# Moving the next pass's k times v products from inside the first MLP to the border between the two MLPs

## The chip, the cores and the metric

One of the cores of a Trainium2 chip runs the whole program. The metric is the time of one execution on the device in microseconds (us); the kernel before is given by the median of three runs.

## What is computed

Linear attention with a norm, and then two MLPs over the same 4608 tokens, all in float32:

```python
kv = np.einsum('bhsd,bhse->bhde', k, v)
out = np.einsum('bhsd,bhde->bhse', q, kv)
out = out / np.sqrt(np.mean(out * out, -1) + 1e-06) * g_norm
x = out.transpose(0, 2, 1, 3).reshape(4608, 512)
x = softplus(x @ w_in) @ moe_w_out                       # 512 -> 2048 -> 512
y = maximum(x @ w1, x @ w2, x @ w3) @ moe2_w_out         # 512 -> 768 -> 512
```

There are 8 batches of 8 heads, 576 tokens and 64 columns a head.

## The kernel before, in words

**Tiling.** The tokens are cut into five passes, each of two column tiles of n = 464 tokens (448 in the last). Each block product of the MLPs is a 2 x 2 block scheme with seven products instead of eight, numbered 1, 5, 6, 2, 7, 4, 3 in the order of their slots. In passes 1 to 4 a factor is split into a high part `hi` (ScalarE, L111) and a remainder `lo` (GpSimd or VectorE, L117), and each product is three matmuls for each half c = 0, 1 of its rows (L127 to L129): six matmuls of 464 columns. Pass 0 multiplies in full float32 (L318), two matmuls a product; beside that it reads the raw float64 weights, converts them (L220 to L231) and stores the split weights for the later passes.

**Order.** `at(t, fn)` puts a step into a list by a time in slots, and one slot is about one product. The list is sorted and recorded; the recording layer under it then sets the order on every engine, and may put an instruction some places before or behind others where nothing forbids it. A pass has eight H groups (first MLP, into the hidden layer, PSUM tiles `Xh`, `Yh`, `Wh`) and eight X groups (out of it, `Xx`, `Yx`, `Wx`), named X00 to X31, seven slots each. X30 starts at base + 98, X31 at base + 105, the second MLP (groups 16 to 24, PSUM tiles `Xo`, `Yo`, `Wo`) at base2 = base + 119. Between them stands `combine_x2` (L639): from the four sums x2 of each half q, it makes the seven right-hand factors. For product 1 only one sum is needed; for product 5 the difference t1 of two of them, for product 6 the difference t2. Product 3 of X30 completes the sums of q = 0, product 3 of X31 those of q = 1.

**The next pass's attention.** `attention_beside` (L539) spreads it over the current pass. For every batch that begins in the first column tile of the next pass (t = 0; one batch in each of the passes 1 to 4) there are four head pairs p: `load_kv` (L400) loads k and v, `kv_mm` (L406) multiplies them, five float32 matmuls of 128 columns into the PSUM tile `kvps` (L412), and `kv_evict` (L414) casts and splits `kvps` into the tiles `kvh`, `kvl` (two casts on ScalarE, two subtracts on VectorE). In the kernel before, `kv_mm` of t = 0 begins at X30's start and has three slots from one pair to the next. A second batch (t = 1, passes 1 and 3) goes into the second MLP at base2 + 16. From base2 + 8 on, `out_mm` multiplies q by `kvh`, `kvl` into the tile `o`.

**Buffers.** k and v tiles have four buffers (L398), so two pairs are loaded ahead, and the third pair's loads wait until the first pair's matmuls are done. Every load and store is issued by SyncE, in one order: weight units `u` and `u3` (four and two buffers), `ux` (one buffer), raw weights, k and v, q. Where one load waits for its buffer, all behind it wait too.

Of the kernel before, what the change touches and what calls it, by code (L numbers as in the profile page):

```python
# [40 lines left out]
def kernel(  # L41
# [99 lines left out]
    def at(t, fn, *args):  # L141
        events.append((t, len(events), fn, args))
# [390 lines left out]
    def new_batches(pas, t):  # L533

        a = TOK[pas] + t * NS[pas]
        first = -1 if a == 0 else (a - 1) // S
        return list(range(first + 1, (a + NS[pas] - 1) // S + 1))

    def attention_beside(pas, t_kv, t0):  # L539

        n = NS[pas]
        for t, tt in ((0, t_kv), (1, t0 + 16)):
            for b in new_batches(pas, t):

                for p in range(NP):
                    at(tt + 3 * p - (10 if p < 2 else 5.85), load_kv, b, p)
                    at(tt + 3 * p + 0.1, kv_mm, b, p)
                at(tt + (9.2 if t == 0 else 10.35), kv_evict, b)
        for k in range(2 * NP):
            h, p = divmod(k, NP)  # L550
            a = TOK[pas] + h * n
            t = t0 + 8 + 6 * k
            at(t - 6, load_q, a, n, p)
            at(t - 3, split_q, a, n, p)
            at(t + 0.3, out_mm, a, n, p)
            at(t + 0.4, square, a, n, p)
            at(t + 4.8, ssq_mm, a, n, p)
            at(t + 4.9, norm, a, n, p)

    def run_pass(pas, base):  # L560
# [24 lines left out]
        start = {name: base + 7 * i for i, name in enumerate(order)}  # L585
# [16 lines left out]
        for fp in range(8):  # L602
            t = start[f"H{fp}"]
# [5 lines left out]
        for n in range(4):  # L609
# [7 lines left out]
            for q in range(2):  # L617
                t = start[f"X{n}{q}"]
# [17 lines left out]
        base2 = base + 7 * len(order) + 7  # L636
# [34 lines left out]
        for k in range(9):  # L671
            fp, j = divmod(k, 3)
            t = base2 + 7 * k
# [4 lines left out]
                                          else (ctile(f"m{w}", N), w == 22))))  # L678
        base3 = base2 + 63
        if pas + 1 < NPASS:  # L680
            attention_beside(pas + 1, start["X30"], base2)
            for s, ms in enumerate(STEPS):
                at(base3 - 2 + SLOT[ms[-1]] + 0.5, combine_x, pas + 1, (s,))

# [33 lines left out]
        t = base3 + 2.05  # L718
# [36 lines left out]
    t = -60  # L755
# [20 lines left out]
    for pas in range(NPASS):  # L776
        bases.append(base)
        base = run_pass(pas, base)
# [80 lines left out]
```

## Time and profile before

| | |
|---|---|
| runs | 1486.07, 1490.92, 1489.62 us, median 1489.62 |
| profiled execution | 1490.04 us, span of the trace 1488.2 |
| busy share of TensorE (PE), VectorE (DVE), ScalarE (ACT), GpSimd (POOL) | 96%, 63%, 56%, 45% |
| mean granted clock of TensorE | 0.991 of full speed |
| DMA | 315.56 MB at 212 GB/s |

Times in the rows are us from the start of the span. Matmuls overlap: one of 464 columns lasts 0.37 us in a row, but in a dense row the next one starts 0.21 us later, and the starts are what counts. A bracket at a row's end is the idle time of the engine before it, and what ended it. A matmul in full float32 is recorded twice.

### The profile page before, as it was taken

Reading aid. Unit: us, or ns where it says so; the run is one execution under the profiler, and the core shown is the slowest. Engines: PE = TensorE matmul, PEld = TensorE weight load, DVE = VectorE, ACT = ScalarE, POOL = GpSimd, SP = SyncE. Lnnn points to the kernel's source line nnn. Section 1 sums busy time; section 2 is a strip of 40 time slices with the busy share of each in tenths; the row PEclk is TensorE's granted clock in tenths of the full one; section 3 lists DMA queues with packets and bytes.
Section 4 is the critical chain, followed back from the end, with each engine's and each line's share of the span. In section 5 each row is a group of like instructions: output and inputs, shape, how many; then the busy total and the mean of one; then the engine's idle time right before and its main releaser. Section 6 shows DMA issues by size and latency. Waiting matters only on the chain.

```text
span 1488.2 us, 18882 instructions
## 1 busy us (share of the span) xinstructions
PE 1427.3 (96%) x6164; PEld 1129.2 (76%) x6164; DVE 933.3 (63%) x1476; ACT 834.5 (56%) x1625; POOL 674.9 (45%) x613
## 2 busy tenths in 40 slices
PE   6898999999999999999999999999999999999999
PEld 4344444555588888778889898888888888898898
DVE  5787887689365676773666556355675554567432
ACT  5676453564197636764866366387636636864321
POOL 3587776643243454451545434434444452534311
PEclk9999999999999999999999999999999999999999
DMA  7657667964366775766566676566665656666572
GB/s 271 250 196 271 213 222 275 324 205 152 120 200 202 220 243 198 263 218 217 186 216 218 228 259 195 168 197 213 217 213 191 201 179 206 203 219 211 188 220 97
DMA packets 107954, 315.56 MB, mean 212 GB/s; under 512 B 12113, under 2 KB 23633, under 8 KB 107857
## 3 DMA queue, kind: packets, MB, share of 16 engines
q1 hardware_dynamic: 107856, 314.36, 63.8%
q8 instruction: 50, 0.82, 0.2%
q14 instruction: 48, 0.39, 0.1%
HBM read 248.78 MB, written 65.54 MB: 211 GB/s over the span
## 4 chain that ended last, share of the span: by engine, by line
PE 72%; DVE 9%; ACT 8%; DMA 4%; issue 4%; POOL 3%; SPq 0%; ACTq 0%; POOLq 0%; DVEq 0%
PE Xo L128 3%; PE Xo L127 3%; PE Xo L318 3%; PE Xo L129 3%; PE Xx L127 3%; PE Xx L129 3%; PE Xx L128 3%; PE Xh L127 3%; PE Xh L129 3%; PE Xh L128 3%; PE oacc L129 3%; PE oacc L128 3%; PE oacc L127 3%; PE oacc L696 3%; PE kvps L412 2%
## 5 line engine op out<-in xcount | busy, mean ns | idle before, releaser
L117 POOL TENSOR_TENSOR lo<-e,hi 128x464 fp32r<-128x464 f32 (+1 forms) x160 | 190.6, 1224 | 201.3 <-ACT hi L111 165.2
L123 POOL TENSOR_TENSOR e<-e 128x464 f32<-128x464 f32 (+1 forms) x40 | 48.2, 1204 | 190.1 <-DVE t L123 172.6
L111 ACT COPY m<-Xo 128x464 f32<-128x464 f32 (+1 forms) x135 | 72.6, 542 | 88.8 <-PE Xo L129 76.9
L117 POOL TENSOR_TENSOR hl<-m,hh 128x464 fp32r<-128x464 f32 (+1 forms) x48 | 58.5, 1222 | 106.2 <-ACT hh L111 106.2
L111 ACT CAST hi<-e 128x464 fp32r<-128x464 f32 (+1 forms) x160 | 87.5, 576 | 21.7 <-PE Yx L128 17.5
L111 ACT CAST hi<-t 128x464 fp32r<-128x464 f32 (+1 forms) x96 | 52.0, 543 | 84.5 <-DVE e L123 38.2
L375 DVE SCALAR_TENSOR_TENSOR e<-h,e 128x464 f32<-128x464 f32 (+1 forms) x80 | 69.5, 871 | 47.1 <-ACT e L374 46.5
L120 DVE TENSOR_TENSOR x<-x,Xx 128x464 f32<-128x464 f32 (+1 forms) x120 | 75.2, 628 | 31.5 <-PE Xx L129 30.1
L374 ACT ACTIVATE e<-e 128x464 f32<-128x464 f32 (+1 forms) x160 | 92.8, 588 | 2.7
L373 ACT ACTIVATE e<-e 128x464 f32<-128x464 f32 (+1 forms) x160 | 92.8, 588 | 2.4
L117 POOL TENSOR_TENSOR u<-sw,u 128x512 fp32r<-128x512 f32 (+1 forms) x76 | 87.9, 1186 | 10.4 <-ACT u L111 10.4
L127 PE MATMUL Xo<-hi,u 128*128 128x464 f32 (+1 forms) x228 | 87.9, 385 | 3.9 <-ACT m L111 3.6
L128 PE MATMUL Xo<-lo,u 128*128 128x464 f32 (+1 forms) x228 | 86.6, 380 | 0.2 <-DVE lo L117 0.2
L220 ACT ACTIVATE cv<-raw 128x512 f32<-128x512 f32 x56 | 35.8, 640 | 90.2 <-DVE sw L231 49.3
L129 PE MATMUL Xo<-hi,u 128*128 128x464 f32 (+1 forms) x228 | 86.1, 378 | 0.0
L123 POOL TENSOR_TENSOR sw<-sw 128x256 f32<-128x256 f32 x75 | 57.1, 762 | 62.0 <-DVE sw L231 45.2
L519 POOL TENSOR_TENSOR og<-og,r 128x464 f32<-128x464 f32 (+1 forms) x32 | 41.0, 1280 | 90.1 <-DVE r L509 82.0
L127 PE MATMUL Xh<-hi,u 128*128 128x464 f32 (+1 forms) x194 | 73.3, 378 | 4.7 <-ACT h L111 4.3
L129 PE MATMUL Xh<-hi,u 128*128 128x464 f32 (+1 forms) x194 | 71.9, 371 | 0.0
L127 PE MATMUL Xx<-hi,u 128*128 128x464 f32 (+1 forms) x192 | 71.8, 374 | 0.0
L128 PE MATMUL Xh<-lo,u 128*128 128x464 f32 (+1 forms) x194 | 71.8, 370 | 0.0
L111 ACT COPY h<-Xh 128x464 f32<-128x464 f32 (+1 forms) x108 | 57.6, 536 | 25.0 <-PE Xh L129 21.4
(229 smaller groups left out, 4330.3 us busy)
## 6 DMA issues: line engine op xcount, KB each, us to landing
u<-wd SPq DMA_DIRECT2D x198, 512.0 KB, 4.3
ux<-wd SPq DMA_DIRECT2D x96, 512.0 KB, 3.4
wd<-u SPq DMA_DIRECT2D x79, 512.0 KB, 3.0
u<-wd SPq DMA_DIRECT2D x106, 256.0 KB, 3.7
raw<-in_w_out_dram SPq DMA_DIRECT2D x22, 512.0 KB, 4.2
k<-in_kp_dram SPq DMA_DIRECT2D x32, 320.0 KB, 5.0
v<-in_vp_dram SPq DMA_DIRECT2D x32, 320.0 KB, 5.3
raw<-in_w_dram SPq DMA_DIRECT2D x18, 512.0 KB, 3.9
```

Of the source, the lines that this page charges most:

```text
L111: nc.scalar.copy(hi, src)
L117: eng_lo.tensor_tensor(out=lo, in0=src, in1=hi.bitcast(F32), op=ALU.subtract)
L120: eng.tensor_tensor(out=o, in0=a, in1=b, op=ALU.add)
L123: eng.tensor_tensor(out=o, in0=a, in1=b, op=ALU.subtract)
L127: nc.tensor.matmul(acc, wh, xh, start=first, stop=False, skip_group_check=on)
L128: nc.tensor.matmul(acc, wh, xl, start=False, stop=False, skip_group_check=on)
L129: nc.tensor.matmul(acc, wl, xh, start=False, stop=last, skip_group_check=on)
L318: nc.tensor.matmul(acc, w[:, c * P:(c + 1) * P], rhs[m, c], start=first and c == 0, stop=c == 1, skip_group_check=not first)
L373: nc.scalar.activation(e, e, AF.Exp, scale=-1.0)
L374: nc.scalar.activation(e, e, AF.Ln, bias=1.0)
L375: nc.vector.scalar_tensor_tensor(out=e, in0=src, scalar=0.0, in1=e, op0=ALU.max, op1=ALU.add)
L696: nc.tensor.matmul(acc[e, t], w[:, o * P:(o + 1) * P], hh[f, t], start=f == 0, stop=f == NF2 - 1)
```

## The change

The first pair of t = 0 now stands at base2 - 6 instead of X30's start (base + 98, which is base2 - 21), and the pairs are two slots apart instead of three. The loads and the eviction move with it: the first two pairs are listed ten slots ahead of their products, the other two behind the product that frees their buffers, the eviction 0.2 slots behind the last product's nominal place. The batch of t = 1 keeps its times.

```diff
-    def attention_beside(pas, t_kv, t0):
+    def attention_beside(pas, t0):
 
         n = NS[pas]
-        for t, tt in ((0, t_kv), (1, t0 + 16)):
+
+        for t, tt, d in ((0, t0 - 6, 2), (1, t0 + 16, 3)):
             for b in new_batches(pas, t):
 
                 for p in range(NP):
-                    at(tt + 3 * p - (10 if p < 2 else 5.85), load_kv, b, p)
-                    at(tt + 3 * p + 0.1, kv_mm, b, p)
-                at(tt + (9.2 if t == 0 else 10.35), kv_evict, b)
+                    at(tt + d * p - (10 if p < 2 else 2 * d - 0.15), load_kv, b, p)
+                    at(tt + d * p + 0.1, kv_mm, b, p)
+                at(tt + 3 * d + (0.2 if t == 0 else 1.35), kv_evict, b)
...
-            attention_beside(pas + 1, start["X30"], base2)
+            attention_beside(pas + 1, base2)
```

TensorE at the border of pass 1, before. `Xx` and `Yx` are the last products of X31 (4 and 3), `Xo`, `Yo` products 1 and 5 of group 16; `u_4127` is the weight unit of product 3.

```order
L129 MATMUL Xo<-hi,ux 128x464
L127 MATMUL o<-qh,kvh_87 128x448
L127 MATMUL Yo<-hi,ux 128x464
L127 MATMUL Xx<-hi,u 128x464
...
L128 MATMUL Yo<-lo,ux 128x464
L129 MATMUL Yo<-hi,ux 128x464
L128 MATMUL o<-ql,kvh_87 128x448
L127 MATMUL Yx<-hi,u_4127 128x464
...
L129 MATMUL o<-qh,kvl_88 128x448
L127 MATMUL o<-qh,kvh_85 128x16
...
L127 MATMUL Xo<-hi,ux 128x464
L127 MATMUL Yo<-hi,ux 128x464
```

The same place in the changed kernel, from the product 4 of X31 on (`u_4103` is now the unit of product 3).

```order
L412 MATMUL kvps<-v,k 128x128 x5
L127 MATMUL Xx<-hi,u 128x464
...
L412 MATMUL kvps<-v,k 128x128 x5
L127 MATMUL Yx<-hi,u_4103 128x464
...
L128 MATMUL Xo<-lo,ux 128x464
L412 MATMUL kvps<-v,k 128x128 x5
L129 MATMUL Xo<-hi,ux 128x464
L127 MATMUL Yo<-hi,ux 128x464
...
L128 MATMUL Yo<-lo,ux 128x464
L129 MATMUL Yo<-hi,ux 128x464
L412 MATMUL kvps<-v,k 128x128 x5
L127 MATMUL Xo<-hi,u 128x464
```

Products 4 and 3 of X31 now come before group 16 starts, and the four k times v blocks stand ahead of product 4, ahead of product 3, inside product 1 and behind product 5 of group 16. The borders of passes 2 and 3 read the same.

SyncE's queue in pass 1 in the changed kernel, behind the loads for X31; `wd_1848` to `wd_1806` are units of groups 16 and 17.

```order
L169 DMA u<-wd_1848 128x1024
L169 DMA u_4276<-wd_1779 128x512
L402 DMA k<-in_kp_dram 128x640
L403 DMA v<-in_vp_dram 128x640
L169 DMA u<-wd_1865 128x1024
L402 DMA k<-in_kp_dram 128x640
L403 DMA v<-in_vp_dram 128x640
L169 DMA u_4358<-wd_1879 128x512
L402 DMA k<-in_kp_dram 128x640
L403 DMA v<-in_vp_dram 128x640
L169 DMA ux<-wd_1806 128x1024
```

The first two k, v pairs here are the third and fourth of the batch; before, they stood among X31's units, six to eight places earlier. The third pair belongs to the next batch.

VectorE at the border of pass 0, before (`cv`, `sw` are the weights' conversion, `x` sums of the first MLP).

```order
L120 TENSOR_TENSOR x_866<-x_866,Xx 128x464
L117 TENSOR_TENSOR kvl_86<-kvps,kvh_85 64x4x64
L120 TENSOR_TENSOR x_870<-x_870,Xx 128x464
L117 TENSOR_TENSOR kvl_86<-kvps,kvh_85 64x4x64
L221 TENSOR_SCALAR cv<-cv 128x512
L120 TENSOR_TENSOR x_842<-x_842,Wx 128x464
```

And in the changed kernel, where the two `kvl` stand behind the difference t2 of q = 1 (`t_1716`) and around a conversion's last step:

```order
L123 TENSOR_TENSOR t_1716<-x_900,t_1715 128x464
L222 TENSOR_SCALAR cv<-cv 128x512
L226 SCALAR_TENSOR_TENSOR cv<-raw,cv 128x512
L117 TENSOR_TENSOR kvl_86<-kvps,kvh_85 64x4x64
L231 SCALAR_TENSOR_TENSOR sw<-raw,cv 128x2x256
L117 TENSOR_TENSOR kvl_86<-kvps,kvh_85 64x4x64
```

The sums of both halves no longer have the subtracts of `kvl` in front of them.

## Rows read from the trace of the kernel before

**Rows 1.** The page's part 4, the chain that ended last by engine.
```profile
PE 72%; DVE 9%; ACT 8%; DMA 4%; issue 4%; POOL 3%; SPq 0%; ACTq 0%; POOLq 0%; DVEq 0%
```
**Rows 2.** Windows: stretch, length, busy (count) of PE, PEld, DVE, ACT, POOL, PEclk, DMA, GB/s.
```profile
208.00:210.60 2.60, 0.74 (x2) 0.00 (x0) 2.60 (x5) 0.63 (x1) 2.60 (x3) 1.00 1.04 405
210.60:215.00 4.40, 4.34 (x11) 2.20 (x12) 4.40 (x8) 0.00 (x0) 3.04 (x3) 1.00 0.64 183
...
239.80:256.64 16.84, 13.87 (x32) 6.35 (x31) 15.43 (x25) 5.39 (x12) 10.48 (x11) 0.90 0.70 251
528.00:548.89 20.89, 20.89 (x119) 19.12 (x119) 10.66 (x19) 5.90 (x12) 10.38 (x9) 1.00 0.84 279
548.89:562.86 13.97, 12.26 (x50) 9.76 (x48) 11.26 (x17) 7.48 (x15) 9.54 (x8) 0.88 0.48 168
831.16:845.51 14.35, 12.60 (x49) 9.48 (x48) 11.38 (x17) 7.50 (x15) 9.94 (x8) 0.88 0.53 177
1107.90:1122.10 14.20, 12.32 (x49) 9.46 (x48) 11.37 (x17) 7.48 (x15) 9.79 (x8) 0.88 0.45 148
```
**Rows 3.** Timeline of TensorE, pass 1: start, duration, engine, line, tile.
```profile
529.28 1.27 PE L412 MATMUL kvps<-v,k 128*128 128x128 f32 x10
...
556.33 0.48 PE L127 MATMUL Xo<-hi,ux 128*128 128x464 f32 x1 [1.25 <-ACT hi L111]
...
557.71 0.68 PE L128 MATMUL Xo<-lo,ux 128*128 128x464 f32 x1 [0.45 <-DVE lo L117]
```
**Rows 4.** The chain of waits in pass 1: start, length, what.
```profile
529.44 1.11 PE kvps L412 x10
...
553.34 2.95 ACT hi L111 x6
...
560.55 0.39 PE Xo L129
...
562.81 0.21 PE Wo L129
```
**Rows 5.** Timeline of TensorE at the border of pass 0.
```profile
238.24 1.72 PE L318 MATMUL Yx<-e,sw 128*128 128x464 f32 x4
...
240.87 1.82 PE L318 MATMUL Xx<-e,sw 128*128 128x464 f32 x4 [0.92 <-DVE x L120]
...
246.31 1.02 PE L318 MATMUL Yo<-t,sw 128*128 128x464 f32 x2 [2.05 <-DVE t L123]
...
259.63 1.72 PE L318 MATMUL Yo<-t,sw 128*128 128x464 f32 x4
```
**Rows 6.** Timeline of VectorE, passes 0 and 1.
```profile
239.86 0.42 DVE L117 TENSOR_TENSOR kvl<-kvps,kvh 64x256 fp32r<-64x256 f32 x1 [2.88 <-ACT kvh L111]
...
560.04 0.64 DVE L117 TENSOR_TENSOR lo<-t,hi 128x464 fp32r<-128x464 f32 x1 [0.61 <-ACT hi L111]
```
**Rows 7.** The tile kvps: all its evictions on ScalarE, duration in ns (least, median, most).
```profile
L111 ACT CAST kvh<-kvps x12: 359/367/368, 239.5 to 1105.2; 64x256 fp32r<-64x256 f32 x12
```
**Rows 8.** Timeline of SyncE's queue: start and length of the issue.
```profile
240.97 3.46 SPq L165 DMA_DIRECT2D wd<-u  x4
...
530.59 0.33 SPq L402 DMA_DIRECT2D k<-in_kp_dram  x1
530.97 0.43 SPq L403 DMA_DIRECT2D v<-in_vp_dram  x1
```
**Rows 9.** DMA issues at 530.97, at 535.9, at 1090.0: size, us from issue to landing.
```profile
v<-in_vp_dram SPq DMA_DIRECT2D x1, 320.0 KB, 3.3
...
v<-in_vp_dram SPq DMA_DIRECT2D x1, 320.0 KB, 5.1
...
v<-in_vp_dram SPq DMA_DIRECT2D x1, 320.0 KB, 6.3
```
**Rows 10.** The page's part 6: all loads of `ux` units and of v, median.
```profile
ux<-wd SPq DMA_DIRECT2D x96, 512.0 KB, 3.4
...
v<-in_vp_dram SPq DMA_DIRECT2D x32, 320.0 KB, 5.3
```

## The prediction

> **What bounds the kernel now.** I read the page's chain first, then windows around each border between the MLPs, then the timelines there. The chain is mostly TensorE [rows 1]: look there for time in which it stands still or runs slowly. In the 20.9 us ahead of the border of pass 1 it is busy without a break, at a granted clock of 1.00, with DMA busy at 0.84 [rows 2]. The k times v blocks of the kernel before lie in that full stretch, so each costs its whole 1.11 us there [rows 4]. From the end of X30's product 3 (548.89, call it **mark 0**) to group 16's product 7 (562.86) the picture turns: PE is busy 12.3 of 14.0 us, the clock is 0.88, DMA falls to 0.48 [rows 2]. The reader is to see two waits in the timeline, on ACT's `hi` and DVE's `lo` [rows 3]; in the chain the six casts that feed product 1's second half end at 556.29, which is mark 7.4; then matmuls follow each other at 0.39 us and later at 0.21 [rows 4], which is the lower of the two clock levels (1.2 GHz against 2.4). Passes 2 and 3 show the same [rows 2].
>
> **The loss at each border.** From mark 0 to group 16's product 7 stand 42 matmuls of 464 columns (seven products) and the `o` pieces, whose columns are worth three more; for their shortness I allow 0.3 us. At 0.21 us that is 45 x 0.21 + 0.3 = 9.75 us of work. The windows last 13.97, 14.35 and 14.20 us [rows 2]: lost are 4.2, 4.6 and 4.45, together **13.3 us**. In pass 0 a matmul in full float32 takes 0.78 us (two from 238.24 to 239.80). From 239.80, the end of X30's product 3, to 259.63 it does 20 of them, 15.6 us, in 19.83 [rows 5]: **4.2 us** lost, by waits of 0.92 and 2.05 us [rows 5] and a clock of 0.90 in most of the stretch [rows 2].
>
> **What the change adds and removes.** No instruction is added or taken away: 20 matmuls, eight loads, two casts and two subtracts per batch move. In passes 1 to 3 all four blocks leave the full stretch, so mark 0 comes 4 x 1.11 = 4.45 us earlier, and the four lie behind it, where 4.2 to 4.6 us were lost. Were nothing else late, product 7 would come at mark 9.75 + 4.45 = 14.2, as late as before, and the whole loss would be won. In pass 0 one pair's block runs long before in either kernel, so three blocks move, 3.3 us, against 4.2 lost.
>
> Is PE then always fed? Product 1's second half wants its `hi` at mark 7.4. Ahead of it PE now has X31's products 7, 4 and 3 (18 matmuls), five of group 16 and three blocks: 23 x 0.21 + 3.33 = mark 8.2. That wait goes. X31's product 3 now ends at mark 6.0, and t1's chain to the cast takes add, subtract and cast, about 0.65 + 0.65 + 0.5, to mark 7.9, also ahead of its use at 8.6. The eviction moves into ACT's row: ahead of the casts of product 2's second half it waits for the last block; behind that block cast, cast and `lo` take 0.37 + 0.5 + 0.64 = 1.5 us [rows 4, 6, 7], while PE has product 6 and the first half of product 2, 10 x 0.21 = 2.1, before it needs that `lo`. Nothing is lost there, with 0.6 us of slack. In pass 0 the evictions leave DVE's row, where they held the sums up for 2.88 us waiting on ACT [rows 6]: those two PE waits go too.
>
> **What is late next: the loads of k and v.** The third pair's buffers come free with the first block. Before, its load had three slots more; now the first block ends at mark 1.26 + 1.11, the k load is issued 1.31 us after that block's start (530.59 against 529.28) and the v load 0.38 later [rows 3, 8], so at mark 2.95. PE wants the pair behind 20 matmuls and two blocks, at mark 6.4. So v may take 3.5 us. It took 3.3 in a quiet queue, 5.1 with unit loads ahead, 6.3 at worst [rows 9]. In the new order a 512 KB and a 256 KB unit load go out 4.2 and 3 us ahead of it, when X31's product 2 (mark -1.3) and X30's product 3 (mark 0) free their buffers; the row nearest to that is the 5.1, which had a 512 KB load 2.7 us ahead. I take 5.1: a wait of **1.6 us** at each of three borders; the ends are 0 and 2.8. The fourth pair is wanted after that wait at about mark 11.4 and its v, issued at 5.3, lands by 11: no second wait (without the first one it would be 0.6). Behind the waiting loads on SP's queue stands group 17's `ux` unit: its buffer comes free behind product 5, at mark 11.4, and its use comes behind product 7, at 14.2 + 6 x 0.21 + 1.6 = 17, 5.6 us against the usual 3.4 [rows 10]. The Trainium skill's page "DMA: Bandwidth & Descriptors" (section "Anatomy of one DMA") gives a fixed cost of about 2.0 us plus bytes at 436 GB/s; by it the two loads of 320 KB would have landed 3.1 us after v's issue and the wait would be nothing, which one of the three rows is near to and two contradict.
>
> In pass 0 only the fourth pair's load comes late. It stands behind a store of a split weight unit, which was issued at 240.97 [rows 8] because GpSimd finished it then; v follows by about 241.75 and, at the usual 5.3 [rows 10], lands at 247.05. PE wants it at (239.80 - 3.33) + 8 x 0.78 + 2.22 = 244.9. So a wait of **2.1 us**, from 0 (should the store go out earlier) to 3.1 (6.3). DVE's `kvl` and the conversion step behind it wait with it, but group 17's sums then still stand some 3 us ahead of PE.
>
> **The sum**, against the profiled execution (1490.04, 0.4 above the median): 13.3 - 3 x 1.6 + 4.2 - 2.1 = 10.6 us less, **1479.5 us**. A wait of 1.9 us ahead of 210.66 left the clock at 1.00 [rows 2], so I charge no clock for waits of 1.6 to 2.1. About 0.3%, 4.5 us, is what a measurement of this kernel can tell from no change.
>
> **The rivals.**
> (a) *The loads land in time.* For it: the 3.3 us row, and DMA at 0.48 in the stretch the loads move to [rows 2]. Against it: the usual v load takes 5.3 [rows 10]. The whole loss goes: 1490 - 17.5 = 1472.5.
> (b) *The wait changes its name.* Loads at the slow end, 2.8 us at three borders and 3.1 in pass 0, and the lower clock still granted behind each of the three (the 3.4 us at 0.39 cost 1.7 us each): 13.3 - 8.4 - 5.1 + 1.1 = 0.9 us less, 1489, no change. For it: at these borders the clock fell after waits of 1.25 and 0.45 us [rows 3]; against it: the new wait is one, with a dense row on both sides.
> (c) *The blocked queue, slower.* SP stands still on the third and fourth pair while unit loads for groups 16 and 17 queue behind them; with (b)'s waits and each border's `ux` unit 2 us late as well, 13.3 - 8.4 - 5.1 - 6 + 1.1 = -5, 1495. It decides only where landings grow beyond 6.3 us, since `ux` has 2.2 us more than its usual landing; DMA's 0.48 speaks against it.
> (d) *It doesn't do what it says:* the recording layer could have put the blocks back. Its order shows them at the border in all four passes, so I give this nothing of its own.
>
> **How the numbers follow.** Forecast 0.55, of which 0.5 faster by over 0.3%: its own ends are 1474 (waits of 0.6 and 0) and 1484 (2.8 and 3.1), and two falls of the clock at the upper end add 3.4; (a) 0.22; (b) 0.18, of which 0.03 still faster; (c) 0.05. Faster by over 0.3%: 0.5 + 0.22 + 0.03 = 0.75; same 0.20; slower 0.05. The range holds the forecast's ends and (a)'s, and reaches up to where (b) begins: 1472 to 1486.5.
>
> **What would show it.** Windows from X30's start to group 16's product 7: the PE waits on `hi` and `lo` gone in passes 1 to 3, one wait on the DMA of v or k in front of the third block instead, 1 to 2 us, clock 1.00. In pass 0 the waits on DVE's sums gone and one of 2 us on the fourth pair. Pass 4's border (no next pass) unchanged. A wait on ACT or DVE at the borders, or half clock in more than one of them, would make the argument wrong; no wait on DMA would make it (a).

## The result, and the profile after

The changed kernel takes **1477.4 us** (median of 4 runs, 1475.2 to 1478.1) against 1490.3 beside it (4 runs, 1486.1 to 1493.6): ratio 0.9916, 95% interval 0.9893 to 0.9938, so 9 to 16 us less. Forecast were 1479.5, range 1472 to 1486.5. The profiled execution took 1477.29 us, its span 1475.5.

The page of the kernel after: busy time by engine, and the chain that ended last by engine, to hold against [rows 1].

```profile
PE 1419.6 (96%) x6164; PEld 1126.5 (76%) x6164; DVE 933.5 (63%) x1476; ACT 835.7 (57%) x1625; POOL 676.5 (46%) x613
...
PE 74%; DVE 8%; ACT 6%; POOL 4%; issue 4%; DMA 3%; SPq 0%; POOLq 0%; ACTq 0%; DVEq 0%
```

TensorE's share of the chain has risen from 72 to 74%, ACT's has fallen from 8 to 6. Where, the windows tell: the three stretches from the end of X30's product 3 (mark 0) to group 16's product 7, as the last three of [rows 2].

```profile
542.20:557.62 15.42, 14.78 (x89) 13.00 (x88) 13.04 (x20) 8.04 (x17) 9.30 (x8) 1.00 0.89 286
818.91:833.77 14.86, 14.18 (x86) 12.36 (x85) 12.30 (x18) 7.41 (x16) 8.97 (x7) 1.00 0.82 273
1092.30:1107.29 14.99, 14.26 (x86) 12.60 (x85) 12.86 (x19) 7.51 (x16) 8.80 (x7) 1.00 0.70 228
```

Each now holds the four blocks, 4.45 us of work more, and is only 1.45, 0.51 and 0.79 us longer than before; the granted clock is 1.00 instead of 0.88. Mark 0 itself comes 4.5 us earlier, counted from the same matmul ahead of the border in both traces. Followed matmul by matmul past the border (in passes 2 and 3 some `o` pieces now stand behind product 7), TensorE gains **2.9, 3.4 and 3.1 us** at the three borders, 9.4 in all.

TensorE's timeline in pass 1: what waits there now, against [rows 3].

```profile
548.92 1.35 PE L412 MATMUL kvps<-v,k 128*128 128x128 f32 x10
...
552.17 0.48 PE L128 MATMUL Xo<-lo,ux 128*128 128x464 f32 x1 [0.49 <-DVE lo L117]
...
553.32 1.27 PE L412 MATMUL kvps<-v,k 128*128 128x128 f32 x10
```

The wait on ACT's `hi` (1.25 us) is gone here; in pass 3 a rest of it stays, ahead of product 5's second half:

```profile
1101.31 0.48 PE L127 MATMUL Yo<-hi,ux 128*128 128x464 f32 x1 [0.25 <-ACT hi L111]
```

The third pair's block starts 0.30 us late (the matmul ahead of it starts at 548.41 and takes 0.21). What remains is a wait on DVE's `lo`; from 551.42, when the matmul ahead of it is through, to 552.17 it costs 0.75 us. It stands in passes 2 and 3 too, with 0.49 and 0.48. The landings of the third pair's v loads (DMA issues at 545.15, 821.85 and 1095.25) are near the shortest of [rows 9]:

```profile
v<-in_vp_dram SPq DMA_DIRECT2D x1, 320.0 KB, 3.6
...
v<-in_vp_dram SPq DMA_DIRECT2D x1, 320.0 KB, 3.7
...
v<-in_vp_dram SPq DMA_DIRECT2D x1, 320.0 KB, 3.2
```

VectorE and, below it, GpSimd in the same place: why `lo` is late.

```profile
543.07 0.65 DVE L123 TENSOR_TENSOR t<-x,x 128x464 f32<-128x464 f32 x1
...
548.40 0.64 DVE L120 TENSOR_TENSOR x<-x,Yx 128x464 f32<-128x464 f32 x1 [0.53 <-PE Yx L129]
549.07 1.50 DVE L123 TENSOR_TENSOR t<-x,x 128x464 f32<-128x464 f32 x1
550.49 1.63 DVE L117 TENSOR_TENSOR lo<-x,hi 128x464 fp32r<-128x464 f32 x1
552.04 0.63 DVE L117 TENSOR_TENSOR lo<-t,hi 128x464 fp32r<-128x464 f32 x1
...
547.75 5.41 POOL L117 TENSOR_TENSOR lo<-x,hi 128x464 fp32r<-128x464 f32 x4 [2.77 <-ACT hi L111]
```

The same `t` takes 0.65 us at 543.07 and 1.50 at 549.07, while GpSimd works through four `lo` subtracts. In this trace DVE has 18 subtracts of these two kinds (`t` from two sums, `lo` from a sum and its `hi`) with two tiles of SBUF as inputs: the 11 that have a GpSimd subtract beside them for most of their time take 0.83 to 1.63 us, the 7 others 0.63 to 0.65. Those with an input in PSUM (548.40, 552.04) keep 0.64 beside GpSimd.

Pass 0 is another matter. From mark 0 (237.03) to the matmul that stood at 259.63 before (259.00) lie 21.97 us, against 19.83 before [rows 5] with three blocks (3.33 us) less in them: 1.2 us won against that profile. But that profile has half clock from 247.2 to 250.6, inside this stretch. The second profile of the kernel before (experiment 2) has none there, and its stretch lasts 18.13. The windows of the first, of the second, and of the changed kernel:

```profile
239.80:259.63 19.83, 16.70 (x38) 7.32 (x37) 17.14 (x28) 7.27 (x15) 13.47 (x13) 0.91 0.66 238
```

```profile
240.57:258.70 18.13, 15.24 (x38) 6.54 (x37) 16.42 (x27) 6.22 (x13) 12.51 (x13) 1.00 0.72 260
```

```profile
237.03:259.00 21.97, 18.24 (x68) 10.02 (x67) 18.19 (x29) 8.96 (x17) 20.04 (x20) 1.00 0.73 255
```

21.97 less 3.33 is 18.64: against the second profile pass 0's border is 0.5 us longer than before. **No gain at this border is shown**; the 1.2 us are the half clock of one profile. TensorE's timeline there:

```profile
241.55 1.82 PE L318 MATMUL Xx<-t,sw 128*128 128x464 f32 x4 [1.68 <-DVE x L120]
...
249.16 1.35 PE L412 MATMUL kvps<-v,k 128*128 128x128 f32 x10 [1.42 <-DMA v<-in_vp_dram]
...
255.81 3.35 PE L318 MATMUL Xo<-x,sw 128*128 128x464 f32 x8 [0.62 <-ACT m L111]
```

The expected wait for v is there, but the wait on DVE's sum has not gone: it is 1.68 us instead of 0.92.

Between these two profiles 9.4 and 1.2 make 10.6, and the spans differ by 12.7. The rest lies where the change moved nothing: half-clock stretches that only one of the two has (before at 653 and 271 us, after at 210 and 1364 us, the last at pass 4's border), and the waits around them. The experiments look at these too.

### The profile page after: what moved, and what is told of

Read it like the earlier page. It is cut to its first block, busy times and chain, and to the rows that moved or that the text cites. A ratio compares the mean times of both kernels' runs of the same rounds, so it can differ in the third digit from the quotient of the medians.

```text
span 1475.5 us, 18888 instructions
## 1 busy us (share of the span) xinstructions
PE 1419.6 (96%) x6164; PEld 1126.5 (76%) x6164; DVE 933.5 (63%) x1476; ACT 835.7 (57%) x1625; POOL 676.5 (46%) x613
## 4 chain that ended last, share of the span: by engine, by line
PE 74%; DVE 8%; ACT 6%; POOL 4%; issue 4%; DMA 3%; SPq 0%; POOLq 0%; ACTq 0%; DVEq 0%
PE Xx L127 3%; PE Xo L128 3%; PE Xx L129 3%; PE Xx L128 3%; PE Xo L129 3%; PE Xo L127 3%; PE Xh L127 3%; PE Xh L129 3%; PE Xh L128 3%; PE Xo L318 3%; PE oacc L697 3%; PE oacc L128 2%; PE oacc L129 2%; PE oacc L127 2%; PE kvps L412 2%
```

## The experiments

Theory: the place makes the gain. At the border a chain of sums, casts and `lo` subtracts holds TensorE up by some 4 us, and blocks that stand there cost little; in X30 and X31 they cost their full time. Rivals: the spacing, or the loads, or accidents of the clock.

**1. The changed kernel again**, and **2. the kernel before again**, no edit.

> The changed kernel once more, unaltered. Theory: the parts of the gain at the borders of passes 1 to 3 (2.9, 3.4 and 3.1 us in the first profile) and the 1.2 us at pass 0's border return within 0.5 us each, while half-clock stretches that lie away from the borders (209.6 and 1362 us in the first profile) depend on the execution and may come, go or move, 1.7 to 2 us each; time 1477 within 2 us. Rival: every clock fall belongs to the kernel; then the two falls stand at the same places and the time is 1477.3 within 0.5 us.

> The kernel before once more, unaltered. Theory: the 3.2 us wait on ACT's m at 653 us (end of pass 1) and the half clock behind it belong to that one profile and not to the kernel: the run with only pass 0's border changed has the old order there and stands 3.5 us further after it. So they are absent here, and PE reaches 665 us some 3 us sooner, counted from the border of pass 1; the four borders lose 4.2, 4.6, 4.45 and 4.2 us again, each within 0.7. Rival: the wait belongs to the old order of pass 1; then it returns with 2.5 to 3.5 us. Time 1489 within 1.5 us, ratio 1.000 within its interval.

Measured: 1476.2 us (5 runs, ratio 0.9918, 0.9903 to 0.9933), and for the kernel before 1487.5 (12 runs, ratio 1.000, 0.9988 to 1.0012). In the second profile of the changed kernel, against the first of the kernel before, the borders give 1.5 us in pass 0 and 2.3, 3.4 and 3.1 in passes 1 to 3, pass 1 a little under what was expected, by a second wait of 0.35 us on a v load. The clock stays at 1.00 at 210 us, where the first profile had a fall behind a like wait; at 1364 us the fall is there again, shorter. So the gains of passes 1 to 3 are the kernel's. Against the second profile of the kernel before the first of the changed one wins 2.6, 3.4 and 3.2 us there, 9.2 in all; in pass 0, counted from X30's start, both of its profiles then lose, 0.5 and 0.2 us. The expected 4.2 us of loss at pass 0's border did not return: its stretch is 1.7 us shorter than in the first profile. The second profile of the kernel before, from pass 1's border on, windows as above, and the end of pass 1:

```profile
547.34:560.98 13.64, 11.52 (x49) 8.54 (x48) 11.26 (x17) 7.48 (x15) 9.22 (x8) 1.00 0.51 177
828.15:842.57 14.42, 12.65 (x50) 9.52 (x48) 11.38 (x17) 7.50 (x15) 10.00 (x8) 0.88 0.49 164
1104.98:1119.22 14.24, 12.36 (x49) 9.48 (x48) 11.37 (x17) 7.48 (x15) 9.82 (x8) 0.88 0.45 145
...
650.00:656.00 6.00, 5.71 (x20) 4.99 (x21) 6.00 (x13) 3.26 (x7) 3.27 (x3) 0.72 0.68 232
```

The first row matters most: the same border with the clock at 1.00 throughout lasts 13.64 us, with the fall 13.97 [rows 2]. **The half clock cost 0.3 us there, not 1.7**: TensorE waits for the chain of casts and subtracts anyway, fast or slow. At pass 0's border, where four records took 3.24 us instead of 1.72 in the half clock, as long a stretch cost 1.7. The wait on ACT's `m` at 650 us is there again, with 2.35 instead of 3.2 us, so the expectation that it was an accident of one profile fell. Experiments 3 and 4 come back to it.

**3. Only pass 0's border moved**, and **4. only those of passes 1 to 3**:

```
-        for t, tt, d in ((0, t0 - 6, 2), (1, t0 + 16, 3)):
+        for t, tt, d in ((0, *((t0 - 6, 2) if pas == 1 else (t0 - 21, 3))), (1, t0 + 16, 3)):   # 3
+        for t, tt, d in ((0, *((t0 - 21, 3) if pas == 1 else (t0 - 6, 2))), (1, t0 + 16, 3)):   # 4
```

> Only pass 0's border has the new place and spacing; passes 1 to 3 have the old. Theory: the border itself gives 1.2 us, and the absent clock fall at 271 us another 2, so the profile is 1.2 to 3.3 us under the kernel before (1487 to 1489 against 1490). Rival: the order at pass 0's border is worth the whole 4.2 us of lost time seen there, so 1486 or less. The borders of passes 1 to 3 keep their waits on ACT's hi and DVE's lo and their clock falls.

> Only the borders of passes 1 to 3 have the new place and spacing; pass 0's has the old. Theory: 9.4 us less by the three borders, up to 2.9 more if the wait on ACT's m at the end of pass 1 stays short and leaves the clock up, and up to 1.6 back at pass 4's border: 1478 to 1482 against 1490. Rival: what the three borders gain is given back behind them, then over 1484.

Measured: pass 0 alone 1485.4 us (12 runs; 0.9976, 0.9965 to 0.9987), passes 1 to 3 alone 1480.0 (6 runs; 0.9940, 0.9926 to 0.9954), beside 1489.3. So 3.9 and 9.3 us, 13.2 together against 13.1 for the whole change on the same chip: the parts add up. Passes 1 to 3 give 2.9, 3.4 and 3.0 at their borders, as in the whole change. Pass 0's time is lower than expected and meets its rival's number (interval 1.9 to 5.2 us), but its border is not where the time is won: against the first profile of before it shows 1.4 us, against the second it loses 0.3. What the profile of experiment 3 does show against that second one is 2.3 us at the end of pass 1, at TensorE's wait on ACT's `m`, which stands behind a cast that waits for a load of stored weights. The row of that wait in both profiles of the kernel before, in experiment 4 and in experiment 3:

```profile
653.31 0.70 PE L127 MATMUL Xo<-hi,u 128*128 128x464 f32 x1 [3.21 <-ACT m L111]
```

```profile
650.29 0.55 PE L127 MATMUL Xo<-hi,u 128*128 128x464 f32 x1 [2.35 <-ACT m L111]
```

```profile
650.55 0.48 PE L127 MATMUL Xo<-hi,u 128*128 128x464 f32 x1 [2.38 <-ACT m L111]
```

```profile
649.85 0.47 PE L127 MATMUL Xo<-hi,u 128*128 128x464 f32 x1 [1.57 <-ACT m L111]
```

The first three are the only profiles with pass 0's blocks at the old place and spacing; in the ten others the wait is 1.23 to 1.87 us. The fall of the clock at pass 4's border, which the change leaves alone, divides them in the same way: these three have none, the ten others all have one, which costs 0.3 to 1.6 us. Behind 300 us the order on every engine is the same in experiment 3 as in the kernel before. So pass 0's part of the gain may arise far behind its border. But the kernel of experiment 6 below wins 2.6 us at the same wait, against the second profile of before, and is no faster by its runs. Where pass 0's part arises is not shown, and its cause stays open.

**5. Without the products**:

```
-            for b in new_batches(pas, t):
+            for b in new_batches(pas, t) if t else ():
```

> Left out: the first half-pass's loads, k times v products and evictions in passes 0 to 3 (t = 0), so the attention there reads older products. This prices the blocks at either place. Theory: before, the 15 moved blocks stood in full stretches and cost 1.11 us each, 16.7 us; without them the borders keep their old waits and clock falls, so the time is 1490 - 16.7 = 1473.4, and the changed kernel pays about 4 us for the same blocks. Rival 1: at the new place they are wholly hidden; then this kernel takes as long as the changed one, 1477 within 1 us. Rival 2: they cost the same at either place and the gain came from elsewhere; then 1477.3 - 16.7 = 1460.6.

Measured: 1467.3 us (4 runs; 0.9860, 0.9844 to 0.9875). None of the three numbers. Beside the runs of 1 and of the kernel before on the same chip, the moved blocks with their loads and evictions cost **22.0 us before and 8.9 us now**. Counted by matmuls, before they cost 4.8, 4.5 and 5.0 us at the borders of passes 1 to 3, which is the 4.45 of the blocks and little else, so that part of the theory holds; now 1.9, 1.1 and 1.9 of it are still paid. The theory failed in pass 0: there they cost 6.4 us beside the first profile of before and 4.7 beside the second, where 3.33 were expected, and 5.1 are still paid. At that border the new place is no cheaper than the old. The three borders without the products, and TensorE in pass 0:

```profile
538.22:551.85 13.63, 11.54 (x49) 8.55 (x48) 11.24 (x17) 7.50 (x15) 9.19 (x8) 1.00 0.51 155
813.04:827.37 14.33, 12.58 (x49) 9.46 (x48) 11.37 (x17) 7.49 (x15) 9.92 (x8) 0.88 0.49 147
1085.30:1098.94 13.64, 11.35 (x50) 8.51 (x49) 11.39 (x17) 7.49 (x15) 9.23 (x8) 1.00 0.49 153
```

```profile
242.58 1.82 PE L318 MATMUL Xx<-t,sw 128*128 128x464 f32 x4 [0.73 <-DVE x L120]
...
249.46 1.04 PE L318 MATMUL Yo<-t,sw 128*128 128x464 f32 x2 [1.03 <-DVE t L123]
```

The windows last about as long as those with the old order (13.6 to 14.3 us): the hole at the border is there whatever stands ahead of it. In pass 3 the clock stays at 1.00 here, and the window lasts 13.64 us instead of 14.20 and 14.24, so half clock costs some 0.6 us there. In pass 0, with no eviction on DVE at all, TensorE still waits 0.73 and 1.03 us for DVE's sums.

**6. The new spacing at the old place**, and **7. the old spacing at the new place**:

```
+        for t, tt, d in ((0, t0 - 21, 2), (1, t0 + 16, 3)):   # 6
+        for t, tt, d in ((0, t0 - 6, 3), (1, t0 + 16, 3)):    # 7
```

> The products two slots apart, but at the old place from X30's start on. Theory: the place makes the gain, not the spacing: each block still costs its 1.11 us in a full stretch, the borders keep their waits on hi and lo and their clock falls, and the closer spacing can add a wait on a load of v: 1490 to 1494. Rival: the spacing makes the gain, by an earlier eviction of kv: 1480 or less.

> The products between the two MLPs, but three slots apart (at -6, -3, 0 and +3 of group 16's start). Theory: only two or three of the four blocks then stand ahead of product 1's second half and the casts, so PE reaches that place about 1.1 us sooner and the wait on hi comes back in part (0.5 to 1 us), the DMA waits go: 1477 to 1481. Rival: the loads decide; with one slot more the third and fourth pair's waits go, pass 0's 1.4 us among them: 1475 or less.

Measured: 1488.6 us (10 runs; 0.9999, 0.9987 to 1.0011) and 1478.8 (4 runs; 0.9929, 0.9906 to 0.9952). The place makes the gain, the spacing none that can be measured. With three slots a small wait on `hi` stands at product 5's second half in each of passes 1 to 3 (0.25, 0.31 and 0.24 us), less than the 0.5 to 1 expected. The borders of passes 1 to 3 give 2.9, 3.1 and 3.1, and pass 0's gives 3.1 instead of 1.2 against the first profile of before (1.4 against the second), because the load of the fourth pair is in time. But most of that is taken back behind it: TensorE waits for GpSimd's `sl` there, as in the changed kernel (1.82 and 1.65 us), and half clock follows (4.97 us for eight records that took 3.28 in experiment 8, and 3.27 in the changed kernel):

```profile
240.72 1.82 PE L318 MATMUL Xx<-t,sw 128*128 128x464 f32 x4 [0.88 <-DVE x L120]
...
253.04 3.35 PE L318 MATMUL Xo<-x,sw 128*128 128x464 f32 x8 [0.48 <-ACT m L111]
...
267.20 0.48 PE L496 MATMUL ss<-sl,ones 128*128 128x464 f32 x1 [1.82 <-POOL sl L117]
267.52 4.97 PE L318 MATMUL Xo<-x,sw 128*128 128x464 f32 x8
```

**8. Own buffers for pass 0's fourth pair**, so that its load need not wait behind a store:

```
+                    own = pas == 1 and t == 0 and p == 3
-                    at(tt + d * p - (10 if p < 2 else 2 * d - 0.15), load_kv, b, p)
+                    at(tt + d * p - (10 if p < 2 or own else 2 * d - 0.15), load_kv, b, p, "raw" if own else False)
...
+        if other == "raw":
+            k, v = (pools["raw"].tile([P, NC, P], F32, tag="kvx", bufs=2, name=i) for i in ("k", "v"))
```

> In pass 0 the fourth pair of k and v gets buffers of its own, so that its load goes out long before and not behind the store of a split weight unit. Theory: the wait of 1.4 us on v in pass 0 goes and nothing takes its place: 1.4 us less than the changed kernel, 1476. Rival: product 1 and 5 of group 16 then wait for DVE's sums instead (0.6 to 1.4 us): 1477, no change.

Measured: 1475.8 us (6 runs; 0.9914, 0.9896 to 0.9932), the same as the changed kernel. The wait on v is gone. In its place, as the rival said but elsewhere, TensorE and then ScalarE:

```profile
255.21 3.35 PE L318 MATMUL Xo<-x,sw 128*128 128x464 f32 x8 [1.99 <-ACT m L111]
```

```profile
253.07 0.62 ACT L111 CAST u<-sw 128x512 fp32r<-128x512 f32 x1 [0.43 <-POOL sw L120]
253.88 0.62 ACT L111 CAST u<-sw 128x512 fp32r<-128x512 f32 x1 [0.19 <-POOL sw L123]
254.52 0.55 ACT L111 COPY m<-Xo 128x464 f32<-128x464 f32 x1
```

ACT's copy `m` stands behind two casts of weights that wait for GpSimd's sums: 1.99 us instead of 0.62. The wait on v hid that one.

**9. GpSimd's two last `lo` later**, **10. the same with ACT's casts left in place**, **11. as 10, and three slots in pass 0**. In 9 the calls are split:

```
-        for q in range(2):
-            at(start[f"X3{q}"] + 12.5, combine_x2, q)
+        at(start["X30"] + 12.5, combine_x2, 0, (0, 1, 2, 3))
+        for q, steps in ((1, (0, 1)), (0, (4,)), (1, (2, 3)), (0, (5,)), (1, (4, 5))):
+            at(start["X31"] + 12.5, combine_x2, q, steps)
```

In 10 `combine` casts the two at once and keeps their subtracts for later:

```
+                if late is not None and m in (4, 3):
+                    cast(nc.scalar, hi, src)
+                    late.append((lo, src, hi.bitcast(F32)))
...
+        at(start["X30"] + 12.5, combine_x2, 0, ALL)
+        at(start["X31"] + 12.5, combine_x2, 1, (0, 1))
+        at(start["X31"] + 12.5, late_lo)
+        at(start["X31"] + 12.5, combine_x2, 1, (2, 3, 4, 5))
```

11 adds `3 if pas == 1 else 2` as the spacing at the new place.

> In passes 1 to 4 GpSimd's last two lo subtracts for the second MLP's first half of the input (products 4 and 3) stand behind those of the second half that come first, so GpSimd has 2 in a row instead of 4 while DVE takes t and lo of the second half. Theory: DVE's t of 1.50 and lo of 1.63 us are slow because GpSimd runs beside them (each reads two tiles from SBUF; others that read PSUM keep 0.64): with GpSimd idle from about 550.5 the lo falls to 0.65, ends 1 us sooner, and the wait on lo at product 1's second half (0.5 us in passes 1 to 3) goes: 1.5 to 2.5 us less than the changed kernel, 1475 to 1476. Rival: they are slow for a cause of their own (bank, operand); lo stays at 1.6 and the time at 1477 or, with GpSimd's lo for products 4 and 3 now late, 1478 to 1480.

> As the run with later lo on GpSimd, but only the two lo subtracts move behind the second half's sum on GpSimd; ACT's casts for products 4 and 3 stay where they are. Theory: GpSimd has 2 lo in a row beside DVE, so DVE's lo takes 0.64 instead of 1.63 us and ends about 1 us sooner, and GpSimd does the two that moved in the time in which it waited for ACT (1.75 us), so nothing is late behind them: the wait on lo at product 1's second half falls below 0.3 us in at least two of passes 1 to 3; 0.5 to 0.75 us each, 1475 to 1476. Rival: as in the earlier run, another order of the matmuls takes it back: 1476 to 1477.5, no change.

> The same, and in pass 0 alone the products stand three slots apart at the new place. Theory: the wait of 1.2 to 1.4 us on the fourth pair's v in pass 0 goes, as in the run with three slots everywhere, where that border gave 3.1 us instead of 1.2 to 1.5, because the last eviction and its wait on PE then stand behind product 2 and not ahead of ACT's copy m; 1.6 us less than the run before it, 1473.5 to 1475, ratio to the kernel before 0.990 or less. Rival: the time won stands before GpSimd's sl at 269 us, which then waits longer: no change, 1475 to 1476.5.

Measured: 1477.5 us (6 runs; 0.9934, 0.9910 to 0.9959), 1478.1 (5 runs; 0.9934, 0.9922 to 0.9946) and 1478.4 (5 runs; 0.9931, 0.9920 to 0.9943). None is faster than the changed kernel. The cause of the slow `lo` is shown nonetheless; DVE in experiment 9, with GpSimd's pair of `lo` from 548.80 to 551.12 and its next operation below:

```profile
550.12 1.51 DVE L123 TENSOR_TENSOR t<-x,x 128x464 f32<-128x464 f32 x1
551.54 0.63 DVE L117 TENSOR_TENSOR lo<-x,hi 128x464 fp32r<-128x464 f32 x1
...
548.80 2.32 POOL L117 TENSOR_TENSOR lo<-x,hi 128x464 fp32r<-128x464 f32 x2 [2.77 <-ACT hi L111]
551.71 1.51 POOL L123 TENSOR_TENSOR x<-x,x 128x464 f32<-128x464 f32 x1 [0.59 <-DVE t L123]
```

`t`, which begins while a `lo` of GpSimd runs, takes 1.51 us. DVE's `lo` begins while GpSimd stands idle and takes 0.63 instead of 1.63; GpSimd's next operation begins 0.17 us later and takes 1.51, where the same one takes 1.18 in the changed kernel. So the one that begins second pays. Why the time didn't fall is in part argued: the recording layer set the matmuls in another order, and the next thing late is a load: in experiment 10 the wait on `lo` at product 1 is gone from passes 1 and 2 (0.23 in pass 3), and TensorE waits for group 17's unit, one row each from passes 1 and 2:

```profile
559.09 0.47 PE L127 MATMUL Xo<-hi,ux 128*128 128x464 f32 x1 [0.55 <-DMA ux<-wd]
...
837.40 0.48 PE L127 MATMUL Xo<-hi,ux 128*128 128x464 f32 x1 [0.99 <-DMA ux<-wd]
```

## Why the prediction was right, point by point

**The full stretch and the hole behind it: right.** Mark 0 came 4.5 us earlier in each of passes 1 to 3, and experiments 5 and 6 show that the blocks cost just that at the old place, whatever their spacing. **How the hole was explained: half wrong.** "The 3.4 us at 0.39 cost 1.7 us each" doesn't hold: with the clock at 1.00 the same border loses 0.3 us less in pass 1 (experiment 2) and 0.6 in pass 3 (experiment 5). The 4.2 to 4.6 us were a chain of sums, casts and `lo`; the low clock lay inside it. The sum came out right because it used the window's length and not its parts. Nor was pass 1's half clock the rule: of the five profiles with the old order at that border one has it.

**The wait for the third pair's v, 1.6 us at each border: mis-sized.** The landing taken, 5.1 us, was 3.6, 3.7 and 3.2, and the waits 0.3, 0.35 and none. In this rival (a) was right, though not in its total: the whole loss did not go. The Trainium skill's fit of 2.0 us and 436 GB/s ("DMA: Bandwidth & Descriptors", "Anatomy of one DMA"), which it gives for transfers issued by GpSimd and not by SyncE, gives, as an estimate, 2.8 us for one load of 320 KB and was the nearer price here; the fourth pair's 5.3 us in pass 1 and 6.1 in pass 0 speak against it.

**A wait that no step had: DVE's `lo`.** "That wait goes", said of product 1, was right for `hi`; by the prediction's own sign, though, a wait on DVE at the borders makes the argument wrong, and one was there in all three. `t1`'s chain to the cast was costed at 0.65 us an operation, and the `lo` behind it was left out. Beside GpSimd `t` took 1.50 and `lo` 1.63: 0.75 us a border; in pass 3 `t1`'s `hi` is late too, by 0.25 in the row and 0.4 by the starts. A row for it stood in the trace of before, a DVE `lo` of the same kind beside GpSimd:

```profile
556.31 1.34 DVE L117 TENSOR_TENSOR lo<-x,hi 128x464 fp32r<-128x464 f32 x1 [0.18 <-ACT hi L111]
```

The Trainium skill has the rule ("SBUF — State Buffer", "Who interferes with whom"): a VectorE operation with two inputs in SBUF and a GpSimd operation that reads SBUF exclude each other, and the later one waits for the other to end. The 18 subtracts above, and experiment 9, agree. Together the waits cost 1.05, 1.1 and 1.2 us instead of three times 1.6: 9.4 us won where 8.5 were forecast. That the two are so near is partly luck: one wait was priced too high, and one not at all.

**Pass 0: the step failed.** Forecast were 2.1 us; at the border nothing is shown to be won (1.2 to 1.5 us against a profile with half clock in it, 0.2 to 0.5 lost against one without). Three things were wrong.

- The loss was counted with 20 matmuls, but X31's products 7, 4 and 3 and group 16's 1, 5, 6, 2, 7 and 4 are 18, 14.0 us: 5.8 us were lost in that profile, of which the half clock was 1.7. Without it 4.1 were lost; in the changed kernel 4.6 are.
- "Those two PE waits go too" fell: the wait on DVE's sum stayed, at 0.9 to 1.7 us, and is there at 0.73 with no evictions at all (experiment 5). DVE's row is full of conversion steps of the weights, not of evictions alone.
- The wait on v came as named, behind the store (242.10, then k and v), 1.4 us long instead of 2.1, but its size is partly chance: v was issued at 242.96 instead of 241.75 and took 6.1 us instead of 5.3, and PE came for it at 247.7 instead of 244.9. Nor was it a price of its own: without it TensorE waits for ACT, or for GpSimd's `sl` (experiments 7 and 8).

By the runs, moving pass 0's blocks alone still saves 1.9 to 5.2 us (experiment 3). Where that arises no step of the prediction says and no run shows, and the cause stays open.

**The forecast of 10.6 us** met 9 to 16. That 9.4 and 1.2 add up to 10.6 as well is a coincidence: passes 1 to 3 gave 0.9 more than forecast, and pass 0 nothing at its border.

**What lies outside the borders** the forecast left out. Part of it comes and goes between executions (210 and 271 us); the wait at 650 us and the fall at pass 4's border go with pass 0's place and spacing in all 13 profiles. So pass 4's border, called unchanged in the prediction, did change in its clock. Between two single profiles all this makes 2 us, as much as a term of the sum.

**Rivals (b) and (c)** fell: the clock stayed at 1.00 at all three borders in each of the eight profiles with the new place there, and in the changed kernel no `ux` unit was late. Experiment 10 shows that (c)'s mechanism is close: with the wait on `lo` gone, `ux` is 0.55 and 0.99 us late.

## What to carry to other kernels

Work that is ready at any time belongs where TensorE waits for a chain of sums and casts, not where it runs full: the window from the last full matmul to the next full row, less the work in it, is the most that such a move can win, here 9.4 of 13.3 us. Pass 0 shows the limit: where the engine that makes the sums is busy itself, the moved work cost as much in the hole (5.1 us) as in the full stretch (4.7). Price a new wait from what the queue does at the new place, and then ask what stands just behind it: here `lo`, `ux`, `m` and `sl` each took over when the wait ahead of them went. Two profiles of the kernel before differ by 3 us in all, 1.7 of them at the very border whose gain was to be read. So count a gain border by border, and against a second profile of the kernel before as well.

## What was not expected of the hardware

- DVE subtracts with two SBUF inputs take 0.63 to 0.65 us alone and up to 1.63 when GpSimd's have begun before them; with an input in PSUM 0.64 either way. A GpSimd operation that begins 0.17 us behind DVE's takes 1.51 instead of 1.18 (experiment 9).
- A border of the same order lasted 13.64 us at a granted clock of 1.00 and 13.97 at 0.88: behind waits of the same size (1.25 and 0.45 us) the clock fell in one execution and not in another. At pass 4's border it fell in ten profiles of 13, behind much the same waits. What decides it stays open.
- Behind a wait of 1.9 us at 210 us one profile of the changed kernel shows a clock fall, the other none. What differs is the wait ahead of it, at 192 us: 0.33 us in the first, with the fall, and 1.47 in the second. All 13 profiles agree: the seven with the fall had waited 0.30 to 0.52 us there, the six without it 1.42 to 1.48. Why the shorter wait goes with the fall is not shown. The row of the wait at 192 and the window at 210, of the first and then of the second:

```profile
192.53 1.79 PE L318 MATMUL Yx<-t,sw 128*128 128x464 f32 x4 [0.33 <-DVE h L120]
```

```profile
207.00:214.00 7.00, 5.08 (x9) 2.04 (x8) 6.41 (x11) 0.64 (x1) 5.56 (x5) 0.76 0.78 258
```

```profile
194.99 1.79 PE L318 MATMUL Yx<-t,sw 128*128 128x464 f32 x4 [1.47 <-DVE h L120]
```

```profile
209.00:214.00 5.00, 3.07 (x8) 1.25 (x7) 5.00 (x8) 0.64 (x1) 5.00 (x5) 1.00 1.01 333
```
